# Decode attention on one core: V chunks through freed K buffers at the end, an output projection spread over the last pair, and two of a weight's four loads moved to a second queue

## The chip, the cores and the metric

The kernel runs on one core of one Trainium2 chip. The metric is the device time of one execution in microseconds (us); lower is better. A profiled execution also gives a span, from the first to the last instruction, which is about 2 us shorter than the device time.

Ratios below are the mean time of one kernel's fast runs over the mean of the other's fast runs of the same rounds, so they are not quite the ratio of the medians that are quoted beside them.

## The reference, cut to what matters

Two sequences each attend with one query to a cache of 32,768 keys and values; 16 query heads share 8 key/value heads of dimension 256. A small feed-forward block and a gate run beside it.

```python
B, Sq, D = 2, 1, 448;  Hq, Hkv, Sk, Dh = 16, 8, 32768, 256
q = x @ wq
p = softmax(einsum(q, k) * Dh**-0.5)        # k, v: (2, 8, 32768, 256) bf16
a = einsum(p, v).reshape(B, Sq, Hq*Dh) @ wo
b = gelu(x @ w1 + b1) @ w2 + b2
g = sigmoid((x * gate_w).sum(-1))
return g * a + (1 - g) * b
```

K and V are 268 MB each. They are read once, 547 MB in all with the weights, and almost nothing is written.

## The kernel before

The work is done pair by pair (16 pairs of batch and key/value head). A pair has 16 chunks of K and 16 chunks of V, 2,048 rows or 1 MB each; partition p of a chunk holds 16 consecutive rows, 8 KB. K chunks go through six buffers (`knat`), loaded from SP's queue. V chunks go through five buffers (`vring`), loaded from ACT's queue. PE transposes K, multiplies with the query, and one pair later multiplies the probabilities with V (P.V); its results go to PSUM, the memory for sums, from which VectorE (DVE) copies them. In the cuts of code "..." stands for lines left out, and some comments are added.

```python
def kslot(i, c):
    gi = i * NCH + c
    return gi % NKB, gi // NKB          # NKB = 6
def vslot(i, c):
    gi = i * NCH + c
    return gi % NVB, gi // NVB          # NVB = 5
...
# SP: small inputs, then wq (into V buffers not yet in use), w1, w2, then all of K
for dc in range(NDC):                   # NDC = 4: 128, 128, 128 and 64 rows of 8 KB
    ...
    sp_.dma_start(wqv[0:r, :], A_wq[dc*128:dc*128+r, :]).then_inc(S["ld_wq"], 16)
...
for i in range(NP):
    for c in range(NCH):
        s, k = kslot(i, c)
        if k >= 1:
            sp_.wait_ge(kfree[s], k)
        ...
        sp_.dma_start(knat[s][:, :, :], src).then_inc(kdma[s], 16)
...
# ACT: one V chunk when its buffer is free
act.wait_ge(vfree[s], k)
...
act.dma_start(vring[s][:, :, :], src).then_inc(vdma[s], 16)
...
# PE, after the last pair: output projection in two halves of 224 columns
def pe_attn_out(half):
    ...
    for h in range(HQ):
        for j in range(2):
            pe.matmul(ps[0:B, MB:MB+DHALF], lhsT=oT_bf[:, h, j, 0:B],
                      rhs=wo_sb[:, h*2+j, half*DHALF:(half+1)*DHALF], ...)
# DVE: copies each half out of PSUM, then out = f + g * (a - f)
```

## Time and profile before

| | before |
|---|---|
| time, median (range, 13 runs) | 1354.48 us (1353.57 to 1355.36) |
| bytes moved | 550.36 MB |
| rate in most slices | 419 GB/s |
| PE busy | 78% of the span |
| from the last V packet to the end of the span | 16.8 us |

These lines are from the profile page of the kernel before. The first two rows cut the span into 40 equal slices of 33.8 us: the busy share of the 16 DMA engines in tenths, and the rate. Then come the DMA queues with packets, MB and the share of engine time (q1 is SP's queue, q10 is ACT's, q8 and q14 fetch instructions), and the chain of waits followed back from the end.

```profile
DMA  9999999999999999999999999999999999999994
GB/s 347 416 413 415 418 419 419 419 419 419 419 419 420 419 419 419 419 403 420 406 419 420 419 418 397 420 419 419 417 409 420 400 419 419 419 419 409 393 380 173
...
q1 hardware_dynamic: 39740, 275.34, 49.2%
q10 hardware_dynamic: 40976, 272.12, 49.1%
q8 instruction: 165, 2.70, 0.8%
q14 instruction: 23, 0.19, 0.0%
...
DMA 79%; PE 14%; DVE 3%; issue 2%; SPq 1%; ACTq 1%; ACT 0%; DVEq 0%
```

The kernel is bound by loads: 419 GB/s slice after slice. The first 17 slices have no dip after the start-up; from the 18th slice on there are dips (403, 406, 397, 409, 400). The last four slices lose rate.

The windows view of the kernel before shows the start and the end more closely. After each stretch come its length, the busy time of each engine with its instruction count, the clock granted to PE, the DMA share and the rate.

```profile
core 0: us, PE busy (x) PEld busy (x) DVE busy (x) ACT busy (x) POOL busy (x), PEclk, DMA share, GB/s
0.00:10.00 10.00, 0.54 (x5) 0.38 (x5) 1.36 (x5) 0.00 (x0) 1.40 (x9) 1.00 0.68 262
10.00:20.00 10.00, 5.33 (x76) 4.83 (x76) 0.00 (x0) 0.00 (x0) 0.00 (x0) 1.00 1.03 336
1275.00:1305.00 30.00, 22.87 (x466) 18.80 (x464) 12.39 (x24) 7.21 (x10) 0.00 (x0) 0.78 0.92 343
1305.00:1322.00 17.00, 7.15 (x112) 2.63 (x112) 0.00 (x0) 0.00 (x0) 0.00 (x0) 0.50 1.01 420
1322.00:1335.00 13.00, 5.11 (x80) 1.88 (x80) 0.00 (x0) 0.00 (x0) 0.00 (x0) 0.50 0.83 345
```

Between 1275 and 1305 us the rate is 343 GB/s. Against 419 that is 76 x 30 / 419 = 5.4 us of transfer that seems to be missing. This is the stretch in which K is used up and only five V buffers are left to load into.

The serial tail is read from the chain of waits in order of time (start, length, what):

```profile
1335.56 1.05 PE ps L529 x16
...
1338.43 0.35 DVE o_sb L640
1338.78 0.14 issue
1338.92 0.99 PE ps L511 x4
...
1340.24 5.29 PE ps L365 x32
1345.53 0.02 issue
1345.56 0.39 DVE a_sb L656
1345.94 0.04 issue
1345.99 3.24 PE ps L365 x32
```

L529 is the last P.V chunk and L365 is the output projection. Nothing overlaps it: 64 matmuls and two copies take from 1340.24 to 1349.67 us.

One more reading is not on the page. The trace has a record of every DMA packet with start and duration, so the number of packets in flight at a moment can be counted. From 50 to 550 us, where the rate is steady, it is 16 for 410 of the 500 us, as many as the page has DMA engines, and one less or up to two more in the rest. A count of engines below is a count of such packets, or of a load's completion times; that each stands for one engine is my reading, as the kept records do not name engines. I shifted these records so that the last packet ends with the span, which is good to about 0.3 us.

```
kernel before, packets of data or instructions in flight
 50 to  550 us: 15 or more in 100% of the time
600 to 1270 us: 9 to 14 for 9.4 us in all, fewer only for moments between packets
1275 to 1305 us: 8 or 9 for a tenth of the time, 7 only for moments
the end: 16 until 1332.0 us, then 8, then 4, last V packet 1335.7 us
```

### The profile page before, as it was taken

What the parts mean: (1) busy time and instruction counts of PE and PEld (TensorE: products, weight loads), DVE (VectorE), ACT (ScalarE), POOL (GpSimd) and SP (SyncE); (2) the same over time, 40 slices, a digit from 0 to 9 for tenths busy, and PEclk for the clock granted to TensorE, in tenths of its full rate; (3) what the DMA queues carried; (4) which work ended last, traced back from release to release, by engine and by line L of the source; (5) the groups of instructions that cost most, each with busy time, mean ns of one, the idle gap of its engine ahead of it and who ended that gap; (6) DMA issues with size and microseconds to landing.
All of it is one profiled execution on the core that took longest, in us unless ns stands there. A gap on an engine that the chain in (4) does not pass through costs nothing.

```text
span 1352.6 us, 45118 instructions
## 1 busy us (share of the span) xinstructions
PE 1059.1 (78%) x20921; PEld 941.8 (70%) x20921; DVE 527.7 (39%) x890; ACT 367.0 (27%) x408; POOL 1.4 (0%) x9
## 2 busy tenths in 40 slices
PE   5987787887877887878878777887778878778865
PEld 4976676777766776777767677777777767668742
DVE  1553443434334343433434334343343434334321
ACT  0333232322223222232322223232232222222210
POOL 0000000000000000000000000000000000000000
PEclk9998987777888788788787878788788778887866
DMA  9999999999999999999999999999999999999994
GB/s 347 416 413 415 418 419 419 419 419 419 419 419 420 419 419 419 419 403 420 406 419 420 419 418 397 420 419 419 417 409 420 400 419 419 419 419 409 393 380 173
DMA packets 80904, 550.36 MB, mean 407 GB/s; under 512 B 8388, under 2 KB 14284, under 8 KB 14732
## 3 DMA queue, kind: packets, MB, share of 16 engines
q1 hardware_dynamic: 39740, 275.34, 49.2%
q10 hardware_dynamic: 40976, 272.12, 49.1%
q8 instruction: 165, 2.70, 0.8%
q14 instruction: 23, 0.19, 0.0%
HBM read 547.43 MB, written 0.00 MB: 405 GB/s over the span
## 4 chain that ended last, share of the span: by engine, by line
DMA 79%; PE 14%; DVE 3%; issue 2%; SPq 1%; ACTq 1%; ACT 0%; DVEq 0%
DMA vring<-in_A_v_cache_dram 75%; PE pst L393 7%; PE ps L529 4%; DMA knat<-in_A_k_cache_dram 3%; PE ps L438 1%; DVE o_tmp L638 1%; SPq L294 1%; ACTq L673 1%; PE ps L511 1%; PE ps L365 1%; DVE o_tmp L636 0%; DVE pm_sb L596 0%; ACT kT L468 0%; DVE kT L471 0%; DVE nb_sb L615 0%
## 5 line engine op out<-in xcount | busy, mean ns | idle before, releaser
L393 PE MATMUL pst<-identb,knat 128*128 128x128 bf16 x8192 | 762.1, 248 | 17.9 <-ACT kT L468 8.7
L471 DVE COPY kT<-pst 128x1024 bf16<-128x1024 bf16 x683 | 465.7, 692 | 725.2 <-PE pst L393 723.6
L393 PEld LDWEIGHTS pst<-identb,knat 128*128 128x128 bf16 x8192 | 569.4, 111 | 84.8 <-issue 75.3
L468 ACT ACTIVATE kT<-pst 128x1024 bf16<-128x1024 bf16 x341 | 348.9, 1023 | 845.1 <-PE pst L393 833.7
L438 PE MATMUL ps<-qT_sb,kT 128*128 128x2 bf16 x8192 | 368.6, 166 | 2.6 <-issue 1.7
L529 PE MATMUL ps<-vring,p_sb 128*2 128x256 bf16 x4096 | 182.1, 304 | 226.6 <-DMA vring<-in_A_v_cache_dram 224.6
L438 PEld LDWEIGHTS ps<-qT_sb,kT 128*128 128x128 bf16 x8192 | 348.1, 102 | 4.1 <-issue 4.1
L529 PEld LDWEIGHTS ps<-vring,p_sb 128*2 128x2 bf16 x4096 | 79.7, 86 | 267.9 <-DMA vring<-in_A_v_cache_dram 251.7
L695 ACT ACTIVATE p_sb<-ps,nb_sb 128x256 bf16<-128x256 f32 x32 | 16.5, 542 | 56.6 <-DVE nb_sb L615 56.6
L511 PE MATMUL ps<-identf,o_sb 2*128 2x2 f32 x64 | 13.4, 309 | 21.2 <-DVE nb_sb L615 18.8
L511 PEld LDWEIGHTS ps<-identf,o_sb 2*128 2x128 f32 x64 | 12.0, 261 | 22.8 <-DVE nb_sb L615 20.0
L636 DVE COPY o_tmp<-ps 2x256 f32<-2x256 f32 x16 | 6.5, 406 | 37.7 <-PE ps L529 37.7
L638 DVE TENSOR_TENSOR o_tmp<-o_tmp,ps 2x256 f32<-2x256 f32 x48 | 20.0, 417 | 1.6
L324 PE MATMUL ps<-xT_sb,vring 128*128 128x2 bf16 (+1 forms) x128 | 9.2, 175 | 10.6 <-DMA vring<-in_A_wq_dram 10.6
L324 PEld LDWEIGHTS ps<-xT_sb,vring 128*128 128x128 bf16 (+1 forms) x128 | 8.3, 106 | 11.5 <-issue 10.7
L596 DVE TENSOR_REDUCE pm_sb<-ps 128x2 f32<-128x512 f32 x16 | 10.9, 681 | 1.0 <-PE ps L438 1.0
L481 PE MATMUL ps<-identf,pm_sb 128*2 128x128 f32 x32 | 6.5, 288 | 5.9 <-DVE pm_sb L596 5.9
L365 PE MATMUL ps<-wo_sb,oT_bf 128*2 128x224 bf16 x64 | 8.5, 305 | 0.8 <-DVE a_sb L656 0.5
L681 ACT ACT_TABLE_LOAD x1 | 1.3, 1283 | 26.8 <-issue 26.8
L365 PEld LDWEIGHTS ps<-wo_sb,oT_bf 128*2 128x2 bf16 x64 | 6.2, 98 | 3.0 <-DVE a_sb L656 0.7
L554 DVE CAST qT_sb<-ps 128x64 bf16<-128x64 f32 x1 | 0.4, 435 | 19.6 <-PE ps L324 19.6
L490 PE MATMUL ps<-dg_sb,ones_f 2*128 2x2 f32 x32 | 6.8, 279 | 0.0
(45 smaller groups left out, 62.4 us busy)
## 6 DMA issues: line engine op xcount, KB each, us to landing
knat<-in_A_k_cache_dram SPq DMA_DIRECT2D x256, 1024.0 KB, 21.5
vring<-in_A_v_cache_dram ACTq DMA_DIRECT2D x256, 1024.0 KB, 23.5
wo_sb<-in_A_wo_dram ACTq DMA_DIRECT2D x1, 3584.0 KB, 86.4
vring<-in_A_wq_dram SPq DMA_DIRECT2D x3, 1024.0 KB, 6.9
w_sb<-in_B_w_dram SPq DMA_DIRECT2D x1, 1568.0 KB, 16.8
w_sb<-in_B_w_dram SPq DMA_DIRECT2D x3, 448.0 KB, 11.9
vring<-in_A_wq_dram SPq DMA_DIRECT2D x1, 512.0 KB, 11.1
w_sb<-in_B_w_dram SPq DMA_DIRECT2D x1, 224.0 KB, 13.1
```

The lines of the kernel that those rows point to most:

```text
L294: sp_.dma_start(knat[s][:, :, :], src).then_inc(kdma[s], 16)
L324: last = pe.matmul(ps[:, col:col + 2], lhsT=wqv[0:r, h * DH + j * 128:h * DH + j * 128 + 128], rhs=xT_sb[0:r, dc, 0:B], start=(dc == 0), s ...
L365: last = pe.matmul(ps[0:B, MB:MB + DHALF], lhsT=oT_bf[:, h, j, 0:B], rhs=wo_sb[:, h * 2 + j, half * DHALF:(half + 1) * DHALF], start=(k2 = ...
L393: last = pe.transpose(tb[:, blk * 128:(blk + 1) * 128], knat[s][:, t, j * 128:(j + 1) * 128], identb[:, :])
L438: last = pe.matmul(ps[:, col:col + 2], lhsT=kT[slot][:, blk * 128:(blk + 1) * 128], rhs=qT_sb[:, b, j, REP * g:REP * g + 2], start=(j == 0 ...
L468: ins = act.activation(out=kT[slot][:, :], in_=tbank(n), func=ACT.Copy)
L471: ins = dve.tensor_copy(out=kT[slot][:, :], in_=tbank(n))
L511: last = pe.matmul(ps[:, MB + 2 * j:MB + 2 * j + 2], lhsT=o_sb[0:2, si, j * 128:(j + 1) * 128], rhs=identf[0:2, 0:2], start=True, stop=True)
L529: last = pe.matmul(ps[32 * gq:32 * gq + 2, base:base + 256], lhsT=p_sb[:, i, (c * T + t) * 2:(c * T + t) * 2 + 2], rhs=vring[s][:, t, :], ...
L638: dch(dve.tensor_tensor(out=o_tmp[0:2, :], in0=o_tmp[0:2, :], in1=ps[32 * gq:32 * gq + 2, base:base + 256], op=ALU.add))
L673: act.dma_start(vring[s][:, :, :], src).then_inc(vdma[s], 16)
L695: v = act_exp.inc(act.activation(out=pv[:, m, :], in_=scv[:, m, :], func=ACT.Exp, bias=nb_sb[:, 2 * si + m:2 * si + m + 1], scale=SCALE, a ...
```

## The change

The change has three parts.

1. The last 17 V chunks alternate between K buffers and V buffers as these come free, so 11 buffers instead of 5 take V at the end. Nine of these loads go out from SP after the last K chunk. The intent is to fill the slow stretch at 1275 to 1305 us.
2. The output projection uses all 448 columns at once, in a PSUM bank that is free by then. The 28 of its 32 matmuls that do not need the last pair run in groups of four behind the last pair's P.V chunks; four remain at the end. The copies out of PSUM go away.
3. Two of the four wq loads (rows 128 to 255, and the last 64 rows) are issued from ACT.

```diff
-    def vslot(i, c):
-        gi = i * NCH + c
-        return gi % NVB, gi // NVB
+    NCK = NP * NCH
+    R0 = NCK - 17
...
+    vmap = {gi: ("R", gi % NVB, gi // NVB, gi - NVB) for gi in range(R0)}
+    cyc = []
+    for x in range(NKB):
+        cyc.append(("K", (NCK - NKB + x) % NKB, None))
+        if x < NVB:
+            cyc.append(("R", (R0 - NVB + x) % NVB, R0 - NVB + x))
...
-            for dc in range(NDC):
+            for dc in range(0, NDC, 2):          # SP; dc = 1, 3 from ACT
...
+            for gi in range(R0, NCK):            # SP, after all of K
+                i, c = divmod(gi, NCH)
+                buf, sd, sf, k, kd, pred = vbuf(i, c)
+                if kd == "K":
+                    ...
+                    sp_.wait_ge(sf, k)
+                    ...
+                    sp_.dma_start(buf[:, :, :], src).then_inc(sd, 16)
...
+        def pe_attn_out(lo, hi):
...
+                for k2 in range(lo, hi):
+                    h, j = divmod(k2, 2)
+                    last = pe.matmul(ps[0:B, AOB:AOB + D], lhsT=oT_bf[:, h, j, 0:B],
+                                     rhs=wo_sb[:, k2, :], start=(k2 == 0), stop=(k2 == 2 * HQ - 1))
...
-        ev(FIN, 4, "pe", "A0", pe_attn_out(0))
...
+        for x in range(7):
+            ev(pv_anchor(NP - 1, 8 + x), 12, "pe", f"PA{x}", pe_attn_out(4 * x, 4 * x + 4))
+        ev(FIN, 4, "pe", "A0", pe_attn_out(28, 32))
```

More of the change, by code (lines that the diff above doesn't have):

```diff
@@ L171, in kslot, with vbuf @@
         return gi % NKB, gi // NKB
-    def vslot(i, c):
-        gi = i * NCH + c
-        return gi % NVB, gi // NVB
+    NCK = NP * NCH
+    R0 = NCK - 17
+    kuse = [(NCK - 1 - s) // NKB + 1 for s in range(NKB)]
+    vuse = [(R0 - 1 - s) // NVB + 1 for s in range(NVB)]
+    vmap = {gi: ("R", gi % NVB, gi // NVB, gi - NVB) for gi in range(R0)}
[4 more added lines that the diff above has]
+            cyc.append(("R", (R0 - NVB + x) % NVB, R0 - NVB + x))
+    last_user = [e[2] for e in cyc]
+    for gi in range(R0, NCK):
+        m = (gi - R0) % len(cyc)
+        kd, s_, _ = cyc[m]
+        use = kuse if kd == "K" else vuse
+        vmap[gi] = (kd, s_, use[s_], last_user[m])
+        use[s_] += 1
+        last_user[m] = gi
+    def vbuf(i, c):
+        kd, s, k, pred = vmap[i * NCH + c]
+        if kd == "K":
+            return knat[s], kdma[s], kfree[s], k, kd, pred
+        return vring[s], vdma[s], vfree[s], k, kd, pred
     def evac_eng(n):
@@ L196, in pv_anchor @@
         return Bq(i) + 6 + GPC * c
-    def vtrig_anchor(i, c):
-        return pv_anchor(i, c) - GPC * (NVB - 1) - 2
     END = NG + LAG + 1
@@ L294, in _ @@
                     sp_.dma_start(knat[s][:, :, :], src).then_inc(kdma[s], 16)
+            for gi in range(R0, NCK):
+                i, c = divmod(gi, NCH)
+                buf, sd, sf, k, kd, pred = vbuf(i, c)
+                if kd == "K":
+                    b, g = pair_bg(i)
+                    sp_.wait_ge(sf, k)
+                    src = A_v_cache[b, g, c * C:(c + 1) * C, :].rearrange("(p t) d -> p t d", p=128)
+                    sp_.dma_start(buf[:, :, :], src).then_inc(sd, 16)
             sp_.wait_ge(S["dve_fin"], 1)
@@ L352, in pe_ffn_f @@
             return fn
-        def pe_attn_out(half):
+        AOB = SC[NP % 2]
+        def pe_attn_out(lo, hi):
             def fn():
-                name = f"A{half}"
-                misc_begin(name)
-                if half == 0:
+                if lo == 0:
                     pe.wait_ge(S["ld_wo"], 16)
-                    pe.wait_ge(S["dve_misc"], misc_k("A0"))
-                last = None
-                k2 = 0
-                for h in range(HQ):
-                    for j in range(2):
-                        last = pe.matmul(ps[0:B, MB:MB + DHALF], lhsT=oT_bf[:, h, j, 0:B],
-                                         rhs=wo_sb[:, h * 2 + j, half * DHALF:(half + 1) * DHALF],
-                                         start=(k2 == 0), stop=(k2 == 2 * HQ - 1))
-                        k2 += 1
-                misc_end(last)
-                if half == 1:
-                    pass
+                    pe.wait_ge(S["dve_misc"], misc_k(f"OT{NP - 2}") + 1)
+                fin = hi == 2 * HQ
+                if fin:
+                    misc_begin("A0")
+                for k2 in range(lo, hi):
+                    h, j = divmod(k2, 2)
+                    last = pe.matmul(ps[0:B, AOB:AOB + D], lhsT=oT_bf[:, h, j, 0:B],
+                                     rhs=wo_sb[:, k2, :], start=(k2 == 0), stop=(k2 == 2 * HQ - 1))
+                if fin:
+                    misc_end(last)
             return fn
@@ L518, in fn @@
             def fn():
-                s, k = vslot(i, c)
+                vt, sd, sf, k, _, _ = vbuf(i, c)
                 if c == 0:
@@ L523, in fn @@
                         pe.wait_ge(S["dve_onorm"], i - 1)
-                pe.wait_ge(vdma[s], 16 * (k + 1))
+                pe.wait_ge(sd, 16 * (k + 1))
                 base = OB[i % 2]
@@ L530, in fn @@
                                      lhsT=p_sb[:, i, (c * T + t) * 2:(c * T + t) * 2 + 2],
-                                     rhs=vring[s][:, t, :],
+                                     rhs=vt[:, t, :],
                                      start=(c == 0 and t < 4), stop=(c == NCH - 1 and t >= T - 4),
                                      tile_position=(0, 32 * gq))
-                last.then_inc(vfree[s], 1)
+                last.then_inc(sf, 1)
             return fn
@@ L627, in fn @@
                 si = i % 2
-                s, k = vslot(i, NCH - 1)
-                dve.wait_ge(vfree[s], k + 1)
+                _, _, sf, k, _, _ = vbuf(i, NCH - 1)
+                dve.wait_ge(sf, k + 1)
                 dve.wait_ge(S["dve_misc"], misc_k(f"RS{i}") + 1)
@@ L651, in dve_ot_step, with dve_a @@
             return fn
-        def dve_a(half):
-            def fn():
-                misc_wait(f"A{half}")
-                misc_done(dve.tensor_copy(out=a_sb[0:B, half * DHALF:(half + 1) * DHALF], in_=ps[0:B, MB:MB + DHALF]))
-                if half == 1:
-                    dve.wait_ge(S["dve_misc"], misc_k("A1") + 1)
-                    dch(dve.tensor_tensor(out=d1_sb[0:B, :], in0=a_sb[0:B, :], in1=f_sb[0:B, :], op=ALU.subtract))
-                    dve.scalar_tensor_tensor(out=fin_bf[0:B, :], in0=d1_sb[0:B, :], scalar=g_sb[0:B, 0:1],
-                                             in1=f_sb[0:B, :], op0=ALU.mult, op1=ALU.add).then_inc(S["dve_fin"], 1)
-            return fn
+        def dve_a():
+            misc_wait("A0")
+            misc_done(dve.tensor_tensor(out=d1_sb[0:B, :], in0=ps[0:B, AOB:AOB + D], in1=f_sb[0:B, :], op=ALU.subtract))
+            dve.wait_ge(S["dve_misc"], misc_k("A0") + 1)
+            dve.scalar_tensor_tensor(out=fin_bf[0:B, :], in0=d1_sb[0:B, :], scalar=g_sb[0:B, 0:1],
+                                     in1=f_sb[0:B, :], op0=ALU.mult, op1=ALU.add).then_inc(S["dve_fin"], 1)
         def act_vtrig(i, c):
@@ L666, in fn @@
                 b, g = pair_bg(i)
-                s, k = vslot(i, c)
+                vt, sd, sf, k, _, _ = vbuf(i, c)
                 if k >= 1:
-                    act.wait_ge(vfree[s], k)
-                elif s < NWQ:
+                    act.wait_ge(sf, k)
+                elif i == 0 and c < NWQ:
                     act.wait_ge(S["pe_misc"], misc_k("Q") + 1)
                 src = A_v_cache[b, g, c * C:(c + 1) * C, :].rearrange("(p t) d -> p t d", p=128)
-                act.dma_start(vring[s][:, :, :], src).then_inc(vdma[s], 16)
+                act.dma_start(vt[:, :, :], src).then_inc(sd, 16)
             return fn
@@ L701, in build_kernel, with act_wq @@
         PRO = -1000
+        def act_wq():
+            for dc in range(1, NDC, 2):
+                r = drows(dc)
+                wqv = vring[dc][:, :, :].rearrange("p t d -> p (t d)")
+                act.dma_start(wqv[0:r, :], A_wq[dc * 128:dc * 128 + r, :]).then_inc(S["ld_wq"], 16)
+        ev(PRO - 2, 12, "act", "WQ", act_wq)
         ev(PRO, 0, "pe", "PRO", pe_prologue)
@@ L710, in build_kernel @@
             for c in range(NCH):
-                a = vtrig_anchor(i, c)
-                _, k = vslot(i, c)
+                _, _, _, k, kd, pred = vbuf(i, c)
+                if kd == "K":
+                    continue
+                a = pv_anchor(pred // NCH, pred % NCH) + 2 if k else None
                 if k == 0:
@@ L747, in build_kernel @@
             ev(oc_anchor[i] + 1, 5, "dve", f"OTr{i}", dve_ot_step(i))
-        ev(FIN, 4, "pe", "A0", pe_attn_out(0))
-        ev(FIN, 5, "dve", "A0r", dve_a(0))
-        ev(FIN + 1, 4, "pe", "A1", pe_attn_out(1))
-        ev(FIN + 1, 5, "dve", "A1r", dve_a(1))
+        for x in range(7):
+            ev(pv_anchor(NP - 1, 8 + x), 12, "pe", f"PA{x}", pe_attn_out(4 * x, 4 * x + 4))
+        ev(FIN, 4, "pe", "A0", pe_attn_out(28, 32))
+        ev(FIN, 5, "dve", "A0r", dve_a)
         events.sort(key=lambda e: (e[0], e[1], e[2]))
```

## The prediction

> **What bounds the kernel.** The DMA engines. The page gives DMA at 9 tenths in 39 of 40 slices and 419 GB/s in the steady ones, and the chain of waits is 79% DMA. PE is 78% busy but waits mostly for loads. In the windows view three places fall short: 0 to 20 us (262, then 336 GB/s), 1270 to 1310 us (383, 319, 360, 388 GB/s; about 5.4 us of transfer missing at 419), and everything after the last V chunk lands near 1335.5 us, a 17 us serial tail (timeline).
>
> **What the change does.**
> 1. Output projection. Before, 64 matmuls of 224 columns in two halves run after everything else: from 1340.24 to 1349.67 us with two copies, 9.4 us on the chain. Now 28 of 32 wide matmuls (448 columns) are slipped behind the last pair's P·V chunks, where PE idles 1.47 us of every 2.48 us; only 4 remain at the end. Estimate from 32 x 224 columns in 3.24 to 5.27 us: 0.8 to 1.3 us. Saves about 8.3 us, all on the chain.
> 2. Half of the wq loads go out from ACT, which has nothing ahead of them, instead of as SP's fifth issue at 2.07 us. [...] the stream starts about 1.3 us earlier; the slow 64-row load (packets 639 ns against 310) now overlaps others. Saves 1.3 to 1.8 us.
> 3. The last 17 V chunks use the freed K buffers too, 9 of them issued on SP. The intent is to fill 1270 to 1310 us. I expect this to give almost nothing. Counting packets in flight in the trace's DMA records, in the dips it is never below 8 of 16 engines, and at the end 8 engines stop near 1332.2 us, the others at 1334 to 1335.5. K packets trickle at 100 GB/s from 1275 to 1287 us. So half of the engines lag (the 165 instruction-fetch packets of about 1.06 us, if spread over those 8, cost each 22 us), and the idle ones are those ahead. For a lagging engine from 1275 to 1303 us, 8.5 V chunks and about 2.4 K chunks at 64 KB per engine and 26.3 GB/s take about 27 of 28 us: it was never starved. [...] so the laggards set the end. Gain 0 to 1 us, against an ideal 5.4.
> 4. Cost: with two queues to the end, chunks 253 and 254 land nearly together 2.5 us before 255, and PE must do two P·V (0.6 to 1.0 us each) and two groups of projection matmuls in that time. Up to 2 us late; I take 0.8. The last K pair's softmax also comes some 4 us later, hidden.
>
> **Sum:** 1354.5 - 8.3 - 1.4 - 0.3 + 0.8 = **1345.3 us**, 80% range 1341 to 1349. Faster by over 2%: 0.01; within 2%: 0.98; slower: 0.01. Even everything together (15 us) is 1.1%.
>
> **What would show it.** Step 1: last wo matmul group of 4, about 1 us, tail after the last load 8 to 10 us. Step 2: wq landed about 1.3 us earlier. Step 3: 1270 to 1310 us back near 415 GB/s, yet the last load lands only 1 to 2 us earlier than 1335.5, with half of the engines done several us before. Step 4: P·V of the last chunks held by PE, not by DMA.
>
> **What would make it wrong.** If the lagging engines did idle in the dips, up to 5 us more (1340). If PE's clock stays at 0.5 in the tail (windows view), the added matmuls could hold the last P·V by 2 to 3 us.

## The result, and the profile after

| | before | after |
|---|---|---|
| time, median | 1354.48 us (13 runs) | 1344.50 us (9 runs, 1344.16 to 1345.86) |
| ratio, 95% interval | | 0.9929 (0.9919 to 0.9938) |
| first large packet | 3.8 us | 2.5 us |
| last V packet | 1335.7 us | 1334.9 us |
| last moment with 12 or more packets in flight | 1332.0 us | 1322.3 us |
| last V packet to end of span | 16.8 us | 7.5 us |

The time is 10.0 us shorter, 0.7%, inside the 2% that was called "same", and 0.8 us from the predicted 1345.3. The lines of the page of the kernel after that answer to those above:

```profile
GB/s 355 416 414 415 419 419 419 418 420 420 419 419 418 420 420 419 418 400 420 408 420 420 418 418 405 420 410 414 419 413 420 398 421 419 418 419 417 416 408 227
...
q1 hardware_dynamic: 40812, 283.21, 50.9%
q10 hardware_dynamic: 39904, 264.26, 48.1%
q8 instruction: 164, 2.69, 0.8%
```

q1 carries 7.9 MB more and q10 as much less: nine V chunks of 1.05 MB that SP now loads, less the 1.6 MB of wq that went to ACT. The 37th to 39th slices rose from 409, 393, 380 to 417, 416, 408. The same windows of the kernel after:

```profile
0.00:10.00 10.00, 0.54 (x5) 0.38 (x5) 1.36 (x5) 0.00 (x0) 1.40 (x9) 1.00 0.81 252
10.00:20.00 10.00, 6.16 (x87) 5.59 (x87) 0.00 (x0) 0.00 (x0) 0.00 (x0) 1.00 1.03 374
1275.00:1305.00 30.00, 21.53 (x409) 18.05 (x407) 11.56 (x21) 6.71 (x9) 0.00 (x0) 0.73 1.00 411
1305.00:1322.00 17.00, 7.91 (x133) 4.20 (x132) 0.32 (x2) 0.50 (x3) 0.00 (x0) 0.60 0.99 399
1322.00:1335.00 13.00, 10.53 (x155) 5.58 (x156) 0.00 (x0) 0.00 (x0) 0.00 (x0) 0.83 0.43 177
```

In the first 20 us the kernel moved (252 + 374) x 10 = 6.3 MB, where before it moved (262 + 336) x 10 = 6.0 MB.

The slow stretch is filled: 343 became 411 GB/s at 1275 to 1305 us. And the rate came off again at 1322 to 1335 us, where 345 became 177 GB/s with a DMA share of 0.43. Counted in bytes moved, the kernel after is 6.1 us ahead at 540 MB and 1.0 us ahead at 550 MB, against 0.7 us at 13 MB. The bytes were moved earlier, and the last of them came as late as before.

The end of the chain of waits, after:

```profile
1332.35 0.61 PE ps L554 x16
...
1334.90 0.47 PE ps L554 x15
...
1337.20 0.35 DVE o_sb L665
1337.55 0.14 issue
1337.68 0.59 PE ps L536 x4
...
1338.52 0.93 PE ps L393 x4
1339.44 0.02 issue
1339.47 0.62 DVE d_sb L680
```

L554 is P.V here. The projection on the chain (L393) is now four matmuls and 0.93 us.

### The profile page after: what moved, and what is told of

Read it like the earlier page. It is cut to its first block, busy times and chain, and to the rows that moved or that the text cites. A ratio compares the mean times of both kernels' runs of the same rounds, so it can differ in the third digit from the quotient of the medians.

```text
span 1342.4 us, 45052 instructions
## 1 busy us (share of the span) xinstructions
PE 1049.2 (78%) x20889; PEld 935.8 (70%) x20889; DVE 526.5 (39%) x888; ACT 367.0 (27%) x408; POOL 1.4 (0%) x9
## 3 DMA queue, kind: packets, MB, share of 16 engines
q8 instruction: 164, 2.69, 0.8%
## 4 chain that ended last, share of the span: by engine, by line
DMA 80%; PE 14%; DVE 3%; issue 2%; ACTq 1%; ACT 0%; SPq 0%; DVEq 0%
DMA vring<-in_A_v_cache_dram 78%; PE pst L418 7%; PE ps L554 3%; PE ps L463 1%; DMA knat<-in_A_k_cache_dram 1%; DVE o_tmp L663 1%; DMA vring<-in_A_wq_dram 1%; ACTq L694 1%; PE ps L351 1%; DVE o_tmp L661 0%; DVE kT L496 0%; PE ps L361 0%; PE ps L536 0%; DVE pm_sb L621 0%; DVE h_sb L585 0%
## 5 line engine op out<-in xcount | busy, mean ns | idle before, releaser
L554 PE MATMUL ps<-vring,p_sb 128*2 128x256 bf16 x3952 | 172.1, 298 | 225.4 <-DMA vring<-in_A_v_cache_dram 223.8
L554 PEld LDWEIGHTS ps<-vring,p_sb 128*2 128x2 bf16 x3952 | 76.2, 85 | 259.6 <-DMA vring<-in_A_v_cache_dram 245.1
L621 DVE TENSOR_REDUCE pm_sb<-ps 128x2 f32<-128x512 f32 x16 | 10.9, 681 | 1.7 <-PE ps L463 1.7
L554 PE MATMUL ps<-knat,p_sb 128*2 128x256 bf16 x144 | 11.2, 359 | 0.0
L393 PE MATMUL ps<-wo_sb,oT_bf 128*2 128x448 bf16 x32 | 8.4, 389 | 0.3 <-DVE oT_bf L674 0.3
L554 PEld LDWEIGHTS ps<-knat,p_sb 128*2 128x2 bf16 x144 | 5.1, 106 | 2.9 <-issue 0.5
```

What stands on the lines that cost most here:

```text
L393: last = pe.matmul(ps[0:B, AOB:AOB + D], lhsT=oT_bf[:, h, j, 0:B], rhs=wo_sb[:, k2, :], start=(k2 == 0), stop=(k2 == 2 * HQ - 1))
L554: last = pe.matmul(ps[32 * gq:32 * gq + 2, base:base + 256], lhsT=p_sb[:, i, (c * T + t) * 2:(c * T + t) * 2 + 2], rhs=vt[:, t, :], start= ...
L621: v = dve_pm.inc(dve.tensor_reduce(out=pm_sb[:, 2 * si:2 * si + 2], in_=scv, axis=AX.X, op=ALU.max))
```

## The experiments

Two theories are to be told apart for part 1. **A**: half of the DMA engines are always behind because they also fetch instructions; they were busy all along, and their work sets the end. **B**: the slow stretch was starvation, and filling it brings 5 us. A third question is whether the parts simply add up.

A summary of all runs that follow, from their own packets (us; times are medians of 4 or 5 runs, of 13 and 9 for before and after; the kernel before had medians of 1354.4 to 1355.2 in all of these; packets in flight were counted every quarter of a microsecond; the tail is the time from the last V packet to the end of the span):

```
run          time      last V packet   12 or more in flight until   from there to last packet   tail
before       1354.48      1335.7              1332.0                        3.7                16.8
after        1344.50      1334.9              1322.3                       12.6                 7.5
aout_only    1346.15      1335.8              1332.0                        3.8                 8.6
wq_only      1352.68      1334.4              1330.8                        3.6                16.5
kbuf_only    1355.08      1337.2              1323.5                       13.7                16.1
no_kbuf      1344.56      1334.5              1331.0                        3.5                 8.0
qk_half      1339.33      1328.9              1316.0                       12.9                 8.5
qkpv_half    1335.86      1326.3              1313.0                       13.3                 7.6
pool10k      1350.74      1341.2              1326.5                       14.7                 7.4
pool20k      1369.48      1361.1              1351.0                       10.1                 7.7
low8         1361.92      1350.6              1336.8                       13.9                 9.6
low8_spread  1359.66      1348.3              1335.3                       13.0                 9.6
wo_8eng      1378.64      1365.5              1351.0                       14.4                 7.4
wo_pairs     1345.51      1336.3              1334.5                        1.8                 8.4
```

### aout_only: the output projection alone

The edit puts part 2 of the diff into the kernel before and nothing else.

> The kernel before with the output projection alone changed (28 of its 32 wide matmuls behind the last P.V chunks, 4 at the end, no copies). Before took 1354.5 us, the whole change 1344.5. My theory: the serial tail alone pays for most of the gain. From the two traces, the last P.V ends 1336.6 us before and 1335.3 after, and from there to the end it is 15.9 us before and 7.0 after. So about 8.5 to 9 us off: 1345.5 to 1346. Last V packet still at 1335.5 to 1336 us. Rival (the filled dips pay): at most 5 us off, 1350 or more.

Measured: 1346.15 us against 1354.46 us in the same rounds, ratio 0.9937 (0.9924 to 0.9949). The last V packet is where it was, 1335.8 us, and the tail went from 16.8 to 8.6 us. The projection alone pays 8.3 us of the 10.

### wq_only: the wq loads alone

The edit puts part 3 into the kernel before.

> The kernel before with only half of the wq loads moved to ACT's queue. The trace after shows the byte count running 0.74 us ahead of before from 8 MB on, and wq landed 0.83 us earlier. Theory: every later byte keeps that lead, so 0.7 to 1.0 us off: about 1353.7. My prediction on record said 1.3 to 1.8 us; the rival is that, with PE's earlier Q giving more: 1352.9.

Measured: 1352.68 us against 1354.46 us, ratio 0.9988 (0.9975 to 1.0002), so between 3.4 us faster and 0.3 us slower. The time does not tell the two expectations apart. The bytes do better: this trace runs 1.1 us ahead of before's from 6 MB on and holds that to the end, with swings between 0.5 and 1.7 us; the trace of the full change had 0.7. One pair of traces is weak evidence for the size, because the start-up varies: the three kept traces with the old start reach 13 MB at 37.7, 38.1 and 38.9 us, the eleven with the new one at 36.6 to 38.1 us, 37.1 on average. So the lead is about 1.1 us, less than the 1.3 to 1.8 that I had predicted, and in this trace it is kept, as theory A needs it.

### kbuf_only and no_kbuf: the K buffers alone, and all but the K buffers

In kbuf_only, parts 2 and 3 are taken out of the changed kernel. In no_kbuf, V goes back to its own five buffers, with parts 2 and 3 kept.

> The kernel before with only the last 17 V chunks spread over K and V buffers. Theory (8 of 16 DMA engines are always behind and never starved): the dips between 1275 and 1305 us fill, the 8 engines ahead finish some 10 us before the others, the last packet lands within 1 us of before's 1335.7, time 1354.0 to 1355.0. Rival (the dips were starvation): 5.4 us of missing transfer come back, 1349 to 1350.

> The changed kernel with the V chunks back in the five V buffers (output projection and wq split kept). Theory: same as the changed kernel within 1 us, 1344 to 1345.5, perhaps a little faster because V chunks land one by one and PE has no backlog at the end (0.3 us). Rival: loses the 5 us, 1349 to 1350.

Measured: kbuf_only 1355.08 us, ratio to before 1.0000 (0.9988 to 1.0013). no_kbuf 1344.56 us, ratio to before 0.9924 (0.9912 to 0.9937), the same as the full change at 0.9929. Two windows of kbuf_only show where the filled stretch went:

```profile
1275.00:1305.00 30.00, 22.03 (x410) 18.84 (x407) 11.26 (x20) 6.14 (x6) 0.00 (x0) 0.69 1.01 414
...
1322.00:1335.00 13.00, 4.24 (x92) 2.45 (x96) 0.00 (x0) 0.00 (x0) 0.00 (x0) 0.63 0.52 217
```

At 1275 to 1305 us it has 414 GB/s where before had 343, and at 1322 to 1335 us 217 where before had 345. Part 1 does exactly what it was meant to do and is worth nothing. Theory B falls. Two expectations of kbuf_only were narrowly missed: its last packet came 1.5 us after before's, not within 1 us, and its time is 0.1 us above the range; its trace was 1.1 us behind before's already at 13 MB. What the summary adds is the count of engines: wherever V goes through K buffers, about half of the engines finish 10 to 15 us before the rest; where it does not, all finish within 4 us of each other. The idle time of the engines ahead was moved from one place to another.

The parts add up within the noise: the ratios of part 2, 3 and 1 alone multiply to 0.9937 x 0.9988 x 1.0000 = 0.9925, and the full change has 0.9929.

That the engines behind were never starved is shown by this pair of runs as far as the time goes: feeding all engines without a gap did not bring the last packet earlier.

### qk_half and qkpv_half: fewer instructions to fetch

This asks why half of the engines are behind. In the kernel after PE has 2 x 20,889 instructions, and queue q8 has 164 packets of 16 KB, or 2.69 MB, which is 64 bytes for each of PE's instructions if q8 carries those alone. The two runs test that too. qk_half leaves out half of the score matmuls, qkpv_half also half of the P.V matmuls. Every load stays. Both change the result. The cut leaves out the start and stop flags, which are adapted.

```diff
-                    for j in range(2):
+                    for j in range(1):          # qk_half: scores
...
-                for t in range(T):
+                for t in range(T // 2):         # qkpv_half: P.V as well
```

> The changed kernel with half of the score matmuls left out (only the first 128 of the 256 head dimensions are summed), so 8,192 fewer PE instructions; result wrong on purpose, every load unchanged. It follows from the GpSimd runs that its fetches went out as a different kind of packet (39 more of 8 KB, in the queue that had 23) and mostly held up one or two engines; the 164 packets of 16 KB match PE's 41,800 instructions alone. Theory: PE's fetches are spread over the 8 engines that lag. 32 packets fewer, 34 us, 4.2 us less on each: 132 packets, the last load lands near 1330.6, time 1340.0 to 1340.8, and the stretch with only 8 engines active shrinks from 12 to about 8 us; the engines ahead still finish near 1322. Rival (the lag of 8 engines is not from fetches): 1344 to 1345, last load at 1334.9.

> As qk_half and also half of the P.V matmuls left out (wrong on purpose): 12,288 fewer PE instructions. Theory: about 116 packets, 6.4 us less on each of the 8 engines, and 0.3 us off the last P.V: 1337.5 to 1338.5. Rival: 1344 to 1345.

Measured: 1339.33 us and 1335.86 us, after 1344.50. The page of qk_half:

```profile
GB/s 360 417 414 415 420 420 420 418 420 421 419 419 420 420 419 420 418 418 421 405 420 420 419 419 399 420 420 419 420 419 420 405 420 420 408 419 420 421 412 215
...
q8 instruction: 132, 2.16, 0.7%
```

132 packets as expected (116 in qkpv_half): 8,192 PE instructions fewer took 32 packets off q8, and 12,288 fewer took 48, which is 256 instructions to a packet of 16 KB both times. So q8 carries PE's instructions. And the last V packet came 6.0 and 8.6 us earlier than in the kernel after. Both times lie below the expected ranges. Fewer PE instructions make the loads end earlier although the data moved are the same. One doubt is left by the times alone: PE also had less to do.

The kept traces go further. The semaphore of each chunk is raised sixteen times while the chunk lands, and the trace keeps the moments. Call the mean of the later eight less the mean of the earlier eight the lag, averaged over the chunks that land within 25 us of a moment:

| | lag at 150 us | lag at 550 us | q8 fetches by 550 us | lag x 8 / fetches | PE busy |
|---|---|---|---|---|---|
| after | 3.1 us | 12.6 us | 68 | 1.48 us | 78% |
| qk_half | 2.5 us | 9.7 us | 55 | 1.41 us | 73% |
| qkpv_half | 2.4 us | 8.5 us | 49 | 1.39 us | 69% |

The lag grows steadily from the start, by about the same 1.4 us for each fetch per lagging engine, if the eight share the fetches, and not in proportion to PE's busy time. The rival, that the lag has nothing to do with fetches, falls. What an instruction does besides being fetched is not separated here; the GpSimd runs below add instructions that touch no data.

The size was off by a third. On eight engines, 6.0 us for 32 packets is 6.0 x 8 / 32 = 1.5 us each, and 8.6 us for 48 packets is 1.4 us each. The packets' own records say 1.07 us. Where the other 0.4 us goes is open.

One expectation failed outright: that the engines ahead would still finish near 1322 us and the stretch with half of them active would shrink to 8 us. They finished at 1316 us, and the stretch is 12.9 us. So the engines ahead do not run freely; their lead is capped. The traces show it: in the kernel after, the lag stops growing and stays between 10.9 and 14.1 us from 600 to 1300 us; in the kernel before, it had shrunk to 7.7 us by 1300 us, so the lead was used up in the slow stretch there. The counts fit that: in the kernel before, no engine idles in the first 550 us, and from the 18th slice on some idle now and then, down to 9 in flight. My reading, not tested by itself: at some lead the eleven buffers are all waiting for the engines behind, and the others stand still; from then on the engines behind set the pace for all.

### pool10k and pool20k: more instructions to fetch

The edit adds waits on GpSimd that are met already:

```diff
             assert ch.n == POOL_DONE
+            for _ in range(10000):              # 20000 in pool20k
+                pool_.wait_ge(S["pool_c"], POOL_DONE)
```

> The changed kernel with 10,000 more instructions on GpSimd, waits that are met already and touch no data. In the trace 165 packets of 16 KB fetch 45,000 instructions, about 1.06 us each. Theory: the same 8 engines fetch all instructions and are the ones behind; 10,000 x 64 bytes are 39 more packets, 41 us in all, 5.2 us on each of 8 engines: 1349.5 us, with the engines that are ahead done at the same 1322 us as now. Rival 1 (the lag has another cause, or fetches spread over 16 engines): 0 to 2.6 us. Rival 2 (other engines fetch for GpSimd, the ones that are ahead): no change.

> The same with 20,000 more instructions: twice the dose. Theory: 78 more packets, 10.3 us on each of 8 engines, 1355 us, if buffers let the lag grow at all; the engines ahead may now be held up by buffers. Rival: 1344.5 to 1350.

The 64 bytes for an instruction can be had from the page of the kernel before: 2.70 MB in q8 for PE's 2 x 20,921 instructions are 64.6 bytes each.

Measured: 1350.74 us (6.2 more than after) and 1369.48 us (25.0 more). The first fits the expectation in size, the second does not, and the mechanism is not the one that I wrote; nor did the engines ahead end at 1322 us in pool10k, but at 1326.5 us. The added waits became 5,000 and 10,000 instructions. Their packets are not in q8, which stayed at 164, but in q14:

```profile
q8 instruction: 164, 2.69, 0.8%
q14 instruction: 62, 0.51, 0.1%
```

That is pool10k, 39 packets of 8 KB more than after's 23, again 64 bytes for each of the 5,000; pool20k has 78 more. They come one every 11.3 us while GpSimd works through its waits, until 443 us in pool10k and until 888 us in pool20k, and just there the rate dips. Between 260 and 450 us of pool10k the number of packets in flight falls to 1 at times; in the kernel after it stays at 15 or more there. The completion counts show how many engines these fetches held up: around 400 us of pool10k fifteen of a chunk's sixteen counts came within 3.0 us of each other, and the last one 13.4 us after them; around 850 us of pool20k it was 2.7 and 14.0 us. So one engine was the slowest; that the others waited on full buffers is my reading. On that reading time is lost only while the burdened engine is further behind than the buffers allow, and the loss need not be in proportion to the dose, as 6.2 and 25.0 us are not. This supports "the engine furthest behind sets the pace" and does not show that the 8 engines are the ones with PE's fetches; qk_half supports that.

### low8, low8_spread and wo_8eng: giving work to half of the engines

If half of the engines have 12 us to spare, a load that only they carry should bring the end forward. I assumed that a transfer of 8 partitions runs on 8 engines; no run had shown it, and the expectations of low8 and wo_8eng still count on it. The trace of wo_8eng agrees in part, with 8 or 9 packets in flight for 23 us between 50 and 130 us. low8 splits V chunks 254 and 255 into 16 transfers of 8 neighbouring partitions, low8_spread into 16 transfers of every sixteenth partition, and wo_8eng does the latter with the wo load, early in the run. The waits count the added transfers.

```diff
-   eng.dma_start(dst[:, :, :], src).then_inc(sd, 16)
+   for r in range(0, 128, 8):                               # low8
+       eng.dma_start(dst[r:r + 8, :, :], src[r:r + 8, :, :]).then_inc(sd, 16)
+   for r in range(16):                                      # low8_spread; wo_8eng for wo
+       eng.dma_start(dst[r::16, :, :], src[r::16, :, :]).then_inc(sd, 16)
```

> The changed kernel with the last two V chunks (254 and 255) each loaded by 16 transfers of 8 partitions[...]. Theory: half the engines carry instruction fetches and set the end, the other half have 12 us to spare (8 active engines from 1322 to 1334 us). If the 8 engines used are the ones with time to spare, the others end 2 x 64 KB or 5 us earlier: 1339.5 to 1340.5. If they are the ones behind, they get 128 KB more each: 1349.5 or more. A mix of both kinds gives something between, near 1349 as well. Rival (all 16 engines are equal and the end is a matter of total bytes): the last two chunks take twice as long at half the engines, 1347 to 1350, with no engine idle before the last 5 us.

> As low8, but each of the 16 transfers of 8 partitions takes every sixteenth partition. In low8 the packets slowed down to half rate (14 engines active at 180 GB/s), as in the 64-row wq load, so writing few neighbouring partitions at once was a cost of its own; spread over the partitions this should be gone. Theory with the 8 engines used being the ones ahead: 1339.5 to 1340.5. With those the ones behind, or a mix: 1349 to 1350, the end showing 8 or fewer engines active for over 15 us. If writing partitions 16 apart is still slow, 1355 or more and it tells nothing about which engines these are.

> The changed kernel with the wo load (4,096 packets of 896 bytes, 10.7 us of each of 16 engines) issued as 16 transfers of 8 partitions, 16 apart[...]. It runs early, between 52 and 112 us, and nobody needs it before the end, so a slow transfer matters less than in the two low8 runs. Theory, if these 8 are the engines that do not fetch PE's instructions: the lagging ones lose 10.7 us of work, the others gain it and have had about 12 us to spare: last load near 1325, time 1334 to 1338. If they are the lagging ones or a mix: 1353 to 1356, dips in the GB/s row from early on. If the small partition count makes it slow as such, the first 150 us lose rate and the time lies between 1346 and 1353 or above, and the question of which engines lag stays open.

Measured: 1361.92, 1359.66 and 1378.64 us. All three are far slower, and none tells which engines are behind. While the small transfers ran, 14 engines were active and moved 183 and 203 GB/s between 1320 and 1334 us. Nine tenths of the 8 KB packets of that time took 480 to 790 ns in low8 and 460 to 720 ns in low8_spread, against 310 ns undisturbed; the wo packets of 896 bytes took 72 ns against 42. The 64-row wq load was slow too, at 639 ns per packet against 310. These transfers have in common that each writes 8 or 64 partitions, not 128; why their packets are slow was not shown. Other sets of 8 partitions were not run, so whether idle engines can be given more work is open.

### wo_pairs: larger packets for wo

The last run tries a small gain that theory A allows: less work for every engine.

```diff
-   A_wo.rearrange("(c p) d -> p c d", p=128)
+   A_wo.rearrange("(h p j) d -> p h (j d)", p=128, j=2)     # into wo_sb as p h (j d)
...
-   lhsT=o_sb[0:2, si, j * 128:(j + 1) * 128]
+   lhsT=o_sb[0:2, si, j:256:2]
```

> The no_kbuf kernel (output projection and wq split, V in its own five buffers; 1344.6 us) with the wo load in runs of two rows: head dimension 2p+j instead of j*128+p on partition p, so 2,048 packets of 1,792 bytes instead of 4,096 of 896. Packets of 896, 3,584 and 8,192 bytes took 41.7, 144 and 310 ns when undisturbed; in between I estimate 76 ns for 1,792, so 9.7 us of each engine instead of 10.7. Theory: every engine's work counts in full, so 1.0 us off: last load 1.0 us earlier than no_kbuf's 1334.45, time 1343.6. Rival (nothing left to gain in the loads): 1344.6. The difference is at the edge of what five rounds can tell.

Measured: 1345.51 us, ratio to before 0.9932 (0.9918 to 0.9945); no_kbuf had 0.9924. The packets took 77 ns as estimated, but the profiled run was 1.3 us behind no_kbuf's already at 13 MB, before wo is loaded, and made up 0.4 us between 40 and 100 MB. Whatever it gains is smaller than what the start-up varies from run to run. No result, and no version here is faster than the changed kernel with a correct sum.

## Why the prediction was right

The predicted time was 1345.3 us and the measured one 1344.5 us. Step by step:

| step | predicted | measured |
|---|---|---|
| output projection off the tail | -8.3 us | -8.3 us alone (aout_only) |
| wq split | -1.4 us | about -1.1 us in bytes, single traces scatter as much; -1.8 us in time, from -3.4 to +0.3 |
| K buffers for V | -0.3 us, 0 to 1 | 0.0 us, from -1.6 to +1.8 (kbuf_only) |
| P.V backlog from two queues | +0.8 us | not seen: 1344.50 against 1344.56 without it |
| sum | -9.2 us | -10.0 us |

That the sum came within 0.8 us is luck in part: a cost that was counted did not occur (step 4), the tail happened to run at a higher clock (step 1), and step 2 gave less than expected. The large term, step 1, and the zero of step 3 are not luck; they were measured one by one.

**Step 1 was right in mechanism and size.** From the last V packet to the end the tail shrank by 8.2 us in aout_only and by 9.3 us in the full change. The tail of 7.5 us is below the 8 to 10 us that were to show this step. The extra microsecond goes with PE's clock: from 1335 to 1342 us of the full change it was granted at 0.87, and the four last matmuls took 0.93 us; in aout_only, from 1336 to 1344 us, it was 0.64, and they took 1.65 us; the DVE pieces of the two tails are equally long. Why the clock differed is not known. The prediction warned of the clock as a danger and did not count it as a gain.

**Step 2 was right in direction, and its size was too large.** The first large packet came 1.3 us earlier, as predicted. The further gain was to come from the 64-row load, which "now overlaps others". It did not. ACT's two loads were nearly done before SP's began: in the trace after, ACT's queue moved 420 GB/s at 4 to 6 us and SP's 2, and from 7 to 9 us the 64-row load still held the total to 210 GB/s. The small inputs in SP's queue suffered too; the first PE matmul moved from 3.2 to 7.7 us, without consequence. wq landed at 13.8 us instead of 14.6 us, 0.8 us earlier. The time from the issue of wq to its first packet is 1.7 us in the trace before (2.07 to 3.8 us).

**Step 3 was the step on which the prediction hung, and it was right.** The obvious reading of the profile was 5.4 us of lost transfer. It was rejected because of three lines of evidence that are all in the trace before: the packets in flight fell to about 8 in the dips and not lower (the record says "never below 8", which was sampled every quarter of a microsecond; a finer count finds 7 for moments), one half of the engines ended later than the other, and a lagging engine had 27 us of work in 28 us. kbuf_only, which fills the dips and gains nothing, shows it. That a load is complete only when its last part has landed was put into the prediction as a rule, without a reading of the trace. The trace of the kernel after shows it for the last V chunk: eight of its sixteen counts had come by 1322.5 us and the last came at 1334.60 us, and PE's P.V of that chunk started at 1334.64 us.

Why the lagging engines lag was put as a condition ("if spread over those 8"). qk_half and qkpv_half support it: 32 and 48 fetches fewer, 6.0 and 8.6 us, and a lag that grows by the same amount per fetch. The size was low: 1.06 us per packet was predicted to cost 22 us on each engine; at the measured 1.45 us it is 164 x 1.45 / 8 = 30 us. That the lead of the other engines is capped was not in the prediction; the lag that stops growing and the failed expectation of qk_half show it. That it is the buffers that cap it was not tested; a run with more or fewer of them would do that.

**Step 4 was wrong, and small.** Chunks 253 and 254 did land close together, 2.3 us before 255 (PE works without a gap from 1332.35 to 1334.6 us), but with the clock granted at 1.00 two P.V and two projection groups together took just these 2.3 us. Ahead of the last P.V, PE's weight loads waited 0.20 us for the load of chunk 255, so it was held by DMA, not by PE. The 0.8 us were not paid.

## What to carry to other kernels

A dip in the load rate is not always starvation (kbuf_only filled this one, from 343 to 414 GB/s, and had a ratio to before of 1.0000): before filling it, ask whether all DMA engines stood still or only those that were ahead; here those that were behind set the end (12.1 us between the eighth and the last count of the last V chunk). The sixteen completion times of each load, kept in the trace, show which it is. Work that does not need the last data should leave the serial tail; here it was 16.8 us, on the chain in full, and easy to size from the trace; 8.2 us of it went in aout_only. In this kernel, bound by loads, the number of instructions was itself a load (32 fetches fewer brought the last V packet 6.0 us earlier), and it was not spread evenly, as far as the lag shows it: at 550 us of the kernel after, the later eight of a chunk's sixteen counts came 12.6 us after the earlier eight on average.
